# Streamed weight parts: one store each instead of four, a third buffer for them, and one buffer fewer for the packing queries

## The chip, the cores and the metric

The kernel runs on one core of a Trainium2 chip. The metric is the device time of one execution in microseconds (us). The clock of TensorE was granted in full over practically the whole execution (mean 0.999).

## The reference

Three stages in float32, one behind the other. `n_pack` is 32, so 8 heads x 32 queries are packed per batch.

```
def sm_attn(qq, kk, vv):                       # softmax attention, scale 1/8
    ...
p_packed = sm_attn(p, k, v)                    # 8 batches, 8 heads, 32 packing queries, 576 keys, 64 wide
x = sm_attn(q, p_packed, p_packed)             # 576 queries per head against 32 packed values
x = x.transpose(0, 2, 1, 3).reshape(4608, 512)
a, b = x @ w1, x @ w2                          # 512 -> 1024
x = ((a * b) @ w3) @ w_out                     # 1024 -> 1024 -> 512
h = x @ w_in                                   # 512 -> 2048
g = where(h >= 1, h, where(h <= -1, 0, (h + 1) ** 2 / 4))
out = g @ w_out2                               # 2048 -> 512
```

The last stage's matrices are called `win` and `wout` in the kernel; weights arrive as 64-bit floating point words.

## The kernel before, in words

TensorE multiplies "high" and "low" halves: each operand is split into a rounded `hi` (ScalarE copies it into a narrower float type) and the rest `lo` (VectorE subtracts), and each product is made of three matmul passes (`PASSES`).

*Batches.* The first part of the kernel (to about 150 us) converts the weights of the second stage and does the attention of batches 0 and 1. Then a loop over `b` = 1 to 7 does the second stage of batch `b` in 24 units: 16 of `ab_unit` (12 matmuls each: a and b, their product on VectorE, split again) and 8 of `x2_unit` (24 matmuls, one copy on ScalarE, one store to DRAM). After certain units (`EARLY`, `LATE`) come the steps of the attention of batch `b + 1`: scores of packing queries against keys (`scores_k`, units 1 and 3), transposes of their exponentials (`turn_e`, 5 and 7), the product with the values (`packed`, 9) and its transpose (`turn_packed`, 10), scores of the 576 queries (`scores_q`, 12 and 14), and so on. The order in which instructions are written is the order on every engine.

*Weight tasks.* After each unit of batches 1 to 6 stands one task out of `weight_tasks()`, 144 in all. They convert the third stage's matrices and make the seven left sides of Strassen's scheme (A11, A22, S1 to S4, A12) from them, in eight groups of 18 tasks: two groups for `win`, two for `wout`, then the same again. So batch 1 starts with a group for `win`, a second one runs from its end into the middle of batch 2, two for `wout` follow to the end of batch 3, and batches 4 to 6 repeat that. A group has four conversions, sums and differences on VectorE, and up to seven parts. `part(i, a)` takes a buffer `hl` out of a ring (`bufs=2`), has ScalarE write `hi` (L632) and VectorE `lo` (L633), and puts a store on a list. Each store is issued on ScalarE's queue two units later by `flush_weights` (L640), ahead of that unit's task.

*Streamed parts.* Left sides in `STREAM` (S4 and A22) of `win` are not kept on the chip but read back later, one chunk of 128 columns at a time, by `ws_load` out of `wst[n]`, laid out `[partition, chunk, which, k, hi or lo, 128]`. Their eight parts are stored in four transfers each, one for a chunk `c`, because the buffer holds all 512 columns of `hi` and then all of `lo`. Parts of other left sides go out in one transfer.

*Packing queries.* `load_p(b)` brings 32 queries per head for `scores_k`; it is issued on SyncE's queue in `turn_packed` of the batch before, behind `load_v`, from a ring of two. `pb` lies on the same side of the on-chip memory as the `hl` ring.

Tile names in the profile: `hl` the parts' buffers, `ws` and `wi` the DRAM copies of streamed and other parts of `win`, `w` those of `wout`, `cvx` the converted weights, `psk` and `psm` PSUM banks, `ta`, `tb`, `g` the steps of `ab_unit`, `st` the copy of `x2_unit`, `big` the softmax tiles, `pp` the scaled packed values, `pb` the packing queries.

Of the kernel before, what the change touches and what calls it, by code (L numbers as in the profile page):

```python
# [8 lines left out]
F32 = mybir.dt.float32  # L9
F32R = mybir.dt.float32r  # L10
# [3 lines left out]
AF = mybir.ActivationFunctionType  # L14
ALU = mybir.AluOpType
# [7 lines left out]
P = 128  # L23
# [10 lines left out]
STREAM = (S4, A22)  # L34
# [23 lines left out]
def fused_kernel(ctx: ExitStack, tc, qT, kT, vv, pb, w1, w2, w3T, wo, win, wout, out):  # L58
    nc = tc.nc
# [6 lines left out]
    wid = [[dram.tile([P, 2, 2, 512], F32, name=f"wi{i}{n}") for n in range(2)] for i in range(7)]  # L66
    wst = [dram.tile([P, 4, 2, 2, 2, P], F32, name=f"ws{n}") for n in range(2)]
    w2d = [dram.tile([P, 8, 256] if i in PLAIN else [P, 8, 2, 256], F32, name=f"w2{i}") for i in range(7)]
# [14 lines left out]
    a2 = tc.alloc_tile_pool(name="a2", bufs=1, side="left", reuse_waits="tile")  # L83
    cv = tc.alloc_tile_pool(name="cv0", bufs=1, side="left", reuse_waits="tile")
# [24 lines left out]
    def load_weight(pool, src, bufs=1):  # L109

        t = pool.tile([P, 512], src.dtype, name="raw", tag="raw", bufs=bufs)
        nc.sync.dma_start(out=t, in_=src)
        return t

    def as_float32(pool, raw, out, bufs=1, act=False):

        if raw.dtype == F32:
            return lambda: None, lambda: None, lambda: nc.vector.tensor_copy(out=out, in_=raw)  # L120
        quarters = raw.bitcast(U16).rearrange("p (n four) -> p n four", four=4)
        t = pool.tile([P, 512], F32, name="cvt", tag="cvt", bufs=bufs)
        halves = out.bitcast(U16).rearrange("p (n two) -> p n two", two=2)

        def scale():
            nc.scalar.activation(  # L126
                out=t, in_=raw.bitcast(F32).rearrange("p (n two) -> p n two", two=2)[:, :, 1],
                func=AF.Copy, scale=2.0 ** -112)
            if act:
                nc.scalar.activation(  # L130
                    out=halves[:, :, 0], in_=quarters[:, :, 1], func=AF.Copy, scale=2.0 ** -13, bias=-4095.5 / 8192)

        def parts():
            if not act:
                nc.vector.tensor_scalar(
                    out=halves[:, :, 0], in0=quarters[:, :, 1], scalar1=13, scalar2=None,
                    op0=ALU.logical_shift_right)
            nc.vector.tensor_scalar(
                out=halves[:, :, 1], in0=quarters[:, :, 3], scalar1=0x8000, scalar2=None, op0=ALU.bitwise_and)

        def join():
            nc.vector.scalar_tensor_tensor(  # L142
                out=out.bitcast(I32), in0=t.bitcast(I32), scalar=3, in1=out.bitcast(I32),
                op0=ALU.logical_shift_left, op1=ALU.bitwise_or)
        return scale, parts, join
# [20 lines left out]
        loaded["q", b] = t  # L166

    def load_p(b):
        t = a2.tile([P, 2, P], F32, name="pb", tag="pb", bufs=2)
        nc.sync.dma_start(out=t, in_=pb[b])  # L170
        loaded["p", b] = t

# [19 lines left out]
    def attention(b, joint=False):  # L192
# [75 lines left out]
        def turn_packed():  # L268
            def pe():
                c["ps"] = psm()  # L270
                nc.tensor.transpose(c["ps"][:, 0, :P], pp, ident)

            def ew():
                c["ppt"] = a2.tile([P, P], F32, name="ppt", tag="ppt", bufs=1)
                nc.scalar.activation(out=c["ppt"], in_=c["ps"][:, 0, :P], func=AF.Copy)
                if 0 < b < B - 1:
                    load_v(b + 1)
                    load_p(b + 1)
            return pe, ew
# [193 lines left out]
    def convert_end(i):  # L473
        parts[i][1]()
        if i:
            parts[i - 1][2]()
        load_part(i + RAW)
        for f, b in LOADS.get(i, ()):
            {"p": load_p, "k": load_k, "v": load_v}[f](b)
# [80 lines left out]
    cv = tc.alloc_tile_pool(name="cv1", bufs=1, side="left", reuse_waits="tile")  # L560
# [12 lines left out]
    w_stores = []  # L573
# [6 lines left out]
    def weight_tasks():  # L580
        groups = []
        for n in range(2):
            groups += [("in", k, n) for k in range(2)]
            groups += [("out", 2 * n + j, 0) for j in range(2)]
        src = []
        for kind, k, n in groups:
            if kind == "in":
                src += [win[(2 * c + k) * P:(2 * c + k + 1) * P, (2 * r + n) * 512:(2 * r + n + 1) * 512]
                        for r, c in ((0, 0), (0, 1), (1, 0), (1, 1))]
            else:  # L590
                src += [wout[r * P:(r + 1) * P, :] for r in (2 * k, 2 * k + 1, 8 + 2 * k, 9 + 2 * k)]
        src += [None] * 3

        def load(s):
            if s is not None:
                raws.append(load_weight(cv, s, 3))
        for s in src[:3]:
            load(s)
        ahead = src[3:]
        tasks = []  # L600
        for kind, k, n in groups:
            x, q = [], {}

            def convert(y, kind=kind, x=x, q=q):
                def f():
                    if y % 2 == 0:
                        x.append(cv.tile([P, 2, 512], F32, name="cvx", tag="cvx", bufs=2))
                    for a, b in ((0, 0), (0, 1), (1, 0), (1, 1)):
                        if kind == "in" and a < len(x):
                            q[10 * a + b + 11] = x[a][:, b]  # L610
                        if kind == "out" and b < len(x):
                            q[10 * a + b + 11] = x[b][:, :, a * 256:(a + 1) * 256]
                    for g in as_float32(cv, raws.pop(0), x[y // 2][:, y % 2]):
                        g()
                    load(ahead.pop(0))
                return f

            def part(i, a, kind=kind, k=k, n=n, q=q):
                def f():
                    if kind == "out" and i in PLAIN:  # L620
                        w_stores.append((2, lambda: nc.scalar.dma_start(out=w2d[i][:, 2 * k:2 * k + 2], in_=q[a])))
                        return
                    p = cv.tile([P, 1024], F32R, name="hl", tag="hl", bufs=2)
                    if kind == "in":
                        v = p.rearrange("p (v n) -> p v n", v=2)
                        hi, lo = v[:, 0], v[:, 1]
                        v = v.bitcast(F32)
                    else:
                        v = p.rearrange("p (j v n) -> p j v n", j=2, v=2)
                        hi, lo = v[:, :, 0], v[:, :, 1]  # L630
                        v = v.bitcast(F32)
                    nc.scalar.activation(out=hi, in_=q[a], func=AF.Copy)  # L632
                    nc.vector.tensor_tensor(out=lo, in0=q[a], in1=hi.bitcast(F32), op=ALU.subtract)  # L633
                    if kind == "out":
                        to = [(w2d[i][:, 2 * k:2 * k + 2], v)]
                    elif i in STREAM:
                        to = [(wst[n][:, c, STREAM.index(i), k], v[:, :, c * P:(c + 1) * P]) for c in range(4)]
                    else:
                        to = [(wid[i][n][:, k], v)]
                    w_stores.append((2, lambda: [nc.scalar.dma_start(out=d, in_=a) for d, a in to]))  # L640
                return f

            def combine(d, a, b, op, q=q):
                return lambda: nc.vector.tensor_tensor(out=q[d], in0=q[a], in1=q[b], op=op)

            tasks += [
                convert(0), convert(1), part(A11, 11), convert(2), convert(3), part(A22, 22),
                combine(22, 21, 22, ALU.add), part(A12, 12), combine(21, 11, 21, ALU.subtract), part(S1, 22),
                combine(22, 22, 11, ALU.subtract), part(S3, 21), None, part(S2, 22),
                combine(12, 12, 22, ALU.subtract), None, part(S4, 12), None,  # L650
            ]
        return tasks
# [259 lines left out]
    w2_t, rawg, op = {}, {}, {}  # L912
# [102 lines left out]
    for s in range(steps):  # L1015
        t, i = divmod(s, 8)
# [186 lines left out]
```

## Time and profile before

| | |
|---|---|
| time, median of 3 runs | 1292.41 us (1288.88 to 1295.26) |
| the profiled execution: own time | 1291.72 us |
| its span, first to last instruction | 1289.6 us (2.1 us lie around it) |
| TensorE matmuls busy | 1252.4 us, 97% |
| VectorE busy | 864.8 us, 67% |
| ScalarE busy | 698.2 us, 54% |
| transfers | 299.47 MB, mean 232 GB/s |

PE is TensorE's matmul, PEld its weight load, DVE is VectorE, ACT ScalarE, SP SyncE; ACTq and SPq are the instructions that issue transfers, which do not count as busy time. L632 is line 632 of the kernel. In brackets behind a row of a timeline stands how long the engine was idle before it, and what released it, by the profile's own inference.

### The profile page before, as it was taken

To read this page: it belongs to the slowest core of one execution; us is meant where nothing else is said; L and a number is where in the kernel's file an instruction comes from. 1 tells how busy PE (TensorE), PEld (TensorE's weight loads), DVE (VectorE), ACT (ScalarE), POOL (GpSimd) and SP (SyncE) were. 2 spreads that over 40 slices of the span, in tenths; PEclk is the share of its full clock that TensorE was granted. 3 is DMA by queue.
4 is the path that set the end of the run, shared out by engine and by line. 5 is a ranking of instruction groups with operands and counts; after the bars stand their busy time and mean duration, and the time that the engine had idled before them with its cause. 6 is when DMAs were issued, how large, how long until landed. Compare 5 with 4: busy or idle time off the path is not lost.

```text
span 1289.6 us, 21585 instructions
## 1 busy us (share of the span) xinstructions
PE 1252.4 (97%) x8312; PEld 1051.7 (82%) x8312; DVE 864.8 (67%) x1422; ACT 698.2 (54%) x1184; POOL 0.7 (0%) x6
## 2 busy tenths in 40 slices
PE   7989999999989999999999999999999999999998
PEld 3468787989888989998888888888878888888888
DVE  4875776768576769535787787877658546464565
ACT  6774444445545454425676766767755443434443
POOL 0000000000000000000000000000000000000000
PEclk9999999999999999999999999999999999999999
DMA  9773566546456542358767686666999868677675
GB/s 339 279 271 134 190 209 193 189 164 238 144 201 196 207 157 101 101 215 320 271 214 281 212 283 235 230 222 239 351 372 340 332 212 288 215 232 289 212 231 177
DMA packets 131798, 299.47 MB, mean 232 GB/s; under 512 B 11632, under 2 KB 54640, under 8 KB 127216
## 3 DMA queue, kind: packets, MB, share of 16 engines
q1 hardware_dynamic: 92752, 242.91, 54.0%
q10 hardware_dynamic: 38944, 55.19, 12.5%
q8 instruction: 65, 1.06, 0.3%
q14 instruction: 37, 0.30, 0.1%
HBM read 196.21 MB, written 101.84 MB: 231 GB/s over the span
## 4 chain that ended last, share of the span: by engine, by line
PE 69%; DVE 10%; ACT 8%; DMA 8%; issue 3%; ACTq 1%; SPq 0%; DVEq 0%
PE x L1127 14%; PE psk L411 12%; PE x L821 11%; PE psk L387 9%; PE z L1127 6%; PE z L821 5%; PE y L1127 4%; PE y L821 3%; PE psk L493 2%; PE psk L187 2%; ACT r L829 1%; DMA wi<-hl 1%; DMA raw<-w 1%; DVE tb L399 1%; ACT r L832 1%
## 5 line engine op out<-in xcount | busy, mean ns | idle before, releaser
L411 PEld LDWEIGHTS psk<-g,w 128*128 128x128 f32 x1536 | 204.7, 188 | 20.7 <-ACT st L438 6.2
L387 PE MATMUL psk<-at,m 128*128 128x288 f32 x1536 | 219.4, 299 | 1.8 <-ACT ta L397 1.5
L387 PEld LDWEIGHTS psk<-at,m 128*128 128x128 f32 x1536 | 207.4, 189 | 14.3 <-issue 8.4
L411 PE MATMUL psk<-g,w 128*128 128x288 f32 x1536 | 211.3, 297 | 5.1 <-ACT st L438 2.7
L821 PE MATMUL x<-x2s,wi 128*128 128x512 f32 (+1 forms) x720 | 163.2, 371 | 1.8 <-ACT m L894 1.2
L983 DVE TENSOR_TENSOR op<-raw,op 128x1024 fp32r<-128x1024 f32 (+1 forms) x94 | 101.8, 1113 | 70.6 <-ACT op L982 70.4
L821 PEld LDWEIGHTS x<-x2s,wi 128*128 128x128 f32 x720 | 125.7, 188 | 27.9 <-ACT m L894 3.9
L982 ACT ACTIVATE op<-raw 128x1024 fp32r<-128x1024 f32 (+1 forms) x94 | 87.4, 966 | 70.6 <-DVE raw L974 32.3
L1127 PE MATMUL x<-op,w 128*128 128x512 f32 (+1 forms) x480 | 100.5, 369 | 0.4 <-DVE op L983 0.3
L1127 PE MATMUL x<-op,hwi 128*128 128x512 f32 (+1 forms) x480 | 100.6, 369 | 0.0
L1127 PEld LDWEIGHTS x<-op,w 128*128 128x128 f32 x480 | 83.8, 188 | 16.3 <-DVE op L983 1.3
L1127 PEld LDWEIGHTS x<-op,hwi 128*128 128x128 f32 x480 | 83.1, 188 | 16.1 <-DVE op L983 0.4
L399 DVE TENSOR_TENSOR tb<-psk,ta 128x288 f32<-128x288 f32 x128 | 57.8, 453 | 54.5 <-ACT ta L397 35.0
L832 ACT ACTIVATE r<-r 128x1024 f32<-128x1024 f32 (+1 forms) x80 | 78.0, 975 | 2.5
L983 DVE TENSOR_TENSOR op<-r,op 128x1024 fp32r<-128x1024 f32 (+1 forms) x46 | 50.2, 1117 | 38.7 <-ACT op L982 38.5
L835 DVE SCALAR_TENSOR_TENSOR U<-U,r 128x512 f32<-128x512 f32 (+1 forms) x80 | 47.4, 634 | 38.3 <-ACT r L832 38.3
L493 PE MATMUL psk<-wo,w3f 128*128 128x512 f32 x128 | 60.2, 621 | 10.9 <-DVE w3f L142 10.8
L894 ACT ACTIVATE m<-x 128x512 f32<-128x512 f32 (+1 forms) x40 | 22.1, 553 | 80.4 <-PE x L821 44.8
L105 ACT ACTIVATE g<-tb 128x288 fp32r<-128x288 f32 x128 | 56.3, 439 | 14.7 <-DVE tb L399 14.7
L126 ACT ACTIVATE cvt<-raw 128x512 f32<-128x512 f32 x72 | 48.7, 676 | 28.3 <-DMA raw<-w3T 7.8
L982 ACT ACTIVATE op<-r 128x1024 fp32r<-128x1024 f32 (+1 forms) x46 | 43.2, 969 | 38.1 <-DVE L L1104 16.2
L397 ACT ACTIVATE ta<-psk 128x288 f32<-128x288 f32 x128 | 51.1, 402 | 21.9 <-PE psk L387 21.8
(111 smaller groups left out, 1858.4 us busy)
## 6 DMA issues: line engine op xcount, KB each, us to landing
raw<-g SPq DMA_DIRECT2D x86, 512.0 KB, 5.2
g<-L SPq DMA_DIRECT2D x64, 512.0 KB, 3.8
r<-g SPq DMA_DIRECT2D x42, 512.0 KB, 5.2
g<-U SPq DMA_DIRECT2D x64, 256.0 KB, 2.1
ws<-ws SPq DMA_DIRECT2D x42, 256.0 KB, 4.3
x2d<-st ACTq DMA_DIRECT2D x72, 144.0 KB, 2.4
v<-vv SPq DMA_DIRECT2D x8, 1280.0 KB, 7.5
wi<-hl ACTq DMA_DIRECT2D x20, 512.0 KB, 3.3
```

What stands on the lines that cost most here:

```text
L105: nc.scalar.activation(out=dst[:, 0], in_=src, func=AF.Copy)
L126: nc.scalar.activation(out=t, in_=raw.bitcast(F32).rearrange("p (n two) -> p n two", two=2)[:, :, 1], func=AF.Copy, scale=2.0 ** -112)
L387: nc.tensor.matmul(ps[w][:, :HS], m_tile[b, w, n][:, s, G, c0 * P:(c0 + 1) * P], at_tile[b][:, G, v, hf * HS:(hf + 1) * HS], start=(k == 0 ...
L397: nc.scalar.activation(out=bs, in_=ps[1][:, :HS], func=AF.Copy)
L399: nc.vector.tensor_tensor(out=g, in0=ps[0][:, :HS], in1=bs, op=ALU.mult)
L411: nc.tensor.matmul(ps, w34[kt][:, s, mt * P:(mt + 1) * P], g_t[kt, hf][:, v, :], start=(kt == kts[0] and n == 0), stop=(kt == kts[-1] and ...
L493: nc.tensor.matmul(acc[4 * hf + m], w3f[hf, j][:, m * P:(m + 1) * P], wof[j], start=(j == 0), stop=(j == 7))
L821: nc.tensor.matmul(bank[s, b][:, :N], w, x2_t[t, q][:, m, k, :N], start=(j == 0 and q in (A11, S1, A12)), stop=(j == 5), skip_group_check= ...
L832: nc.scalar.activation(out=r, in_=r, func=AF.Square)
L982: nc.scalar.activation(out=o[:, :, 0, :N], in_=a[0], func=AF.Copy)
L983: nc.vector.tensor_tensor(out=o[:, :, 1, :N], in0=a[0], in1=o[:, :, 0, :N].bitcast(F32), op=ALU.subtract)
L1127: nc.tensor.matmul(bank[b][d][:, :N], w2_t[q][j // 2][:, 2 * (j % 2) + k, s, d * P:(d + 1) * P], op[x][:, k, v, :N], start=start and k == ...
```

## The change

Three edits. The buffer of a streamed part is laid out chunk by chunk (128 columns of `hi`, then the same 128 of `lo`, four times), both split instructions write it so, and it is stored in one transfer with four runs of 1 KB per partition. The ring `hl` has three buffers, not two. The ring `pb` has one, not two.

```
     def load_p(b):
-        t = a2.tile([P, 2, P], F32, name="pb", tag="pb", bufs=2)
+        t = a2.tile([P, 2, P], F32, name="pb", tag="pb", bufs=1)
...
-                    p = cv.tile([P, 1024], F32R, name="hl", tag="hl", bufs=2)
-                    if kind == "in":
+                    p = cv.tile([P, 1024], F32R, name="hl", tag="hl", bufs=3)
+                    whole = q[a]
+                    if kind == "in" and i in STREAM:
+                        v = p.rearrange("p (c v n) -> p c v n", c=4, v=2)
+                        hi, lo = v[:, :, 0], v[:, :, 1]
+                        whole = whole.rearrange("p (c n) -> p c n", c=4)
+                        v = p.bitcast(F32).rearrange("p (c n) -> p c n", c=4)
+                    elif kind == "in":
...
-                    nc.scalar.activation(out=hi, in_=q[a], func=AF.Copy)
-                    nc.vector.tensor_tensor(out=lo, in0=q[a], in1=hi.bitcast(F32), op=ALU.subtract)
+                    nc.scalar.activation(out=hi, in_=whole, func=AF.Copy)
+                    nc.vector.tensor_tensor(out=lo, in0=whole, in1=hi.bitcast(F32), op=ALU.subtract)
                     if kind == "out":
-                        to = [(w2d[i][:, 2 * k:2 * k + 2], v)]
+                        to = w2d[i][:, 2 * k:2 * k + 2]
                     elif i in STREAM:
-                        to = [(wst[n][:, c, STREAM.index(i), k], v[:, :, c * P:(c + 1) * P]) for c in range(4)]
+                        to = wst[n][:, :, STREAM.index(i), k].rearrange("p c v n -> p c (v n)")
                     else:
-                        to = [(wid[i][n][:, k], v)]
-                    w_stores.append((2, lambda: [nc.scalar.dma_start(out=d, in_=a) for d, a in to]))
+                        to = wid[i][n][:, k]
+                    w_stores.append((2, lambda: nc.scalar.dma_start(out=to, in_=v)))
```

## Rows read from the trace of the kernel before

**Rows 1.** The chain of work that ended last, by engine, share of the span.

```profile
PE 69%; DVE 10%; ACT 8%; DMA 8%; issue 3%; ACTq 1%; SPq 0%; DVEq 0%
```

**Rows 2.** Busy time by stretch: PE, PEld, DVE, ACT, POOL; clock, DMA share, GB/s.

```profile
151.00:510.00 359.00, 344.84 (x3399) 313.27 (x3398) 264.28 (x555) 176.97 (x408) 0.00 (x0) 1.00 0.54 186
...
184.00:211.00 27.00, 27.00 (x238) 23.89 (x237) 22.43 (x42) 13.20 (x27) 0.00 (x0) 1.00 0.42 133
278.00:309.10 31.10, 31.10 (x349) 28.79 (x349) 23.12 (x55) 17.86 (x44) 0.00 (x0) 1.00 0.60 206
340.00:374.00 34.00, 30.47 (x337) 27.23 (x336) 24.42 (x56) 17.66 (x43) 0.00 (x0) 1.00 0.76 249
243.00:263.00 20.00, 18.38 (x156) 16.50 (x154) 16.08 (x34) 9.00 (x19) 0.00 (x0) 1.00 0.61 210
```

**Rows 3.** Timeline of TensorE: start, duration, what, [idle before, releaser].

```profile
171.08 0.33 PE L271 MATMUL psm<-ident,pp 128*128 128x128 f32 x1 [1.57 <-DVE pp L262]
...
181.58 12.96 PE L411 MATMUL psk<-g,w 128*128 128x288 f32 x96 [0.86 <-ACT ta L397]
...
224.76 1.45 PE L228 MATMUL psm<-ident,big 128*116 128x128 f32 x8 [2.15 <-ACT big L212]
...
246.72 8.46 PE L411 MATMUL psk<-g,w 128*128 128x288 f32 x62 [0.24 <-ACT ta L397]
...
262.93 6.61 PE L411 MATMUL psk<-g,w 128*128 128x288 f32 x48 [1.38 <-ACT st L438]
...
361.59 0.33 PE L271 MATMUL psm<-ident,pp 128*128 128x128 f32 x1 [0.84 <-DVE pp L262]
...
369.53 3.46 PE L387 MATMUL psk<-at,m 128*128 128x288 f32 x24 [1.49 <-ACT ta L397]
374.05 1.19 PE L411 MATMUL psk<-g,w 128*128 128x288 f32 x7 [1.05 <-ACT ta L397]
...
416.31 1.09 PE L228 MATMUL psm<-ident,big 128*116 128x128 f32 x8 [1.24 <-ACT big L212]
```

**Rows 4.** Timeline of ScalarE (ACT) and its queue (ACTq), same columns.

```profile
164.50 2.85 ACTq L640 DMA_DIRECT2D ws<-hl  x3
167.40 0.63 ACT L632 ACTIVATE hl<-cvx 128x512 fp32r<-128x512 f32 x1 [2.61 <-DMA ws<-hl]
...
169.22 0.34 ACTq L640 DMA_DIRECT2D wi<-hl  x1
...
176.08 0.63 ACT L632 ACTIVATE hl<-cvx 128x512 fp32r<-128x512 f32 x1 [3.03 <-DMA wi<-hl]
...
216.54 1.85 ACTq L640 DMA_DIRECT2D ws<-hl  x2
...
219.50 0.63 ACT L632 ACTIVATE hl<-cvx 128x512 fp32r<-128x512 f32 x1 [2.18 <-issue]
...
243.65 2.01 ACTq L640 DMA_DIRECT2D ws<-hl  x4
...
368.55 0.63 ACT L632 ACTIVATE hl<-cvx 128x512 fp32r<-128x512 f32 x1 [4.99 <-DMA wi<-hl]
```

**Rows 5.** Instructions by tile: duration ns min/median/max, first and last start us.

```profile
L632 ACT ACTIVATE hl<-cvx x40: 614/630/652, 154.7 to 503.3; 128x512 fp32r<-128x512 f32 x40
...
L640 ACTq DMA_DIRECT2D ws<-hl x32: 377/500/1572, 164.1 to 435.1; - x32
...
L664 SPq DMA_DIRECT2D f<-x2d x5: 518/530/615, 522.3 to 827.2; - x5
```

**Rows 6.** Transfers: queue, count, KB each, median us from issue to landing.

```profile
wi<-hl ACTq DMA_DIRECT2D x20, 512.0 KB, 3.3
...
ws<-hl ACTq DMA_DIRECT2D x32, 128.0 KB, 2.1
```

**Rows 7.** Timelines of TensorE and SyncE's queue (SPq): packing queries.

```profile
153.63 0.72 PE L187 MATMUL psm<-qk,pb 64*32 64x288 f32 x16 [0.48 <-ACT big L212]
...
168.15 0.45 SPq L170 DMA_DIRECT2D pb<-pb  x1
```

## The prediction

> **What bounds the kernel now.** I read the chain of waits first, then the engines by stretch, then TensorE's own timeline wherever it stands still, and last ScalarE's timeline just before those places. The chain says that TensorE carries 69% of the span, and VectorE, ScalarE and transfers some 8 to 10% each [rows 1]: matmuls set the time, except at spots where another engine holds them up. The change touches only the weight tasks of batches 1 to 6, which run from 151 to 510 us. There TensorE is busy for 344.8 of 359.0 us [rows 2]. So 14.2 us of its idle time are all that can be won; what leaves ScalarE, VectorE or a queue elsewhere is worth nothing.
>
> Eleven of these idle spells (12.4 us) stand in six places [rows 3]; I name them by batch. A is batch 1 (171.08, 181.58), B and C batch 2 (224.76; 246.72 and 262.93), D batch 4 (361.59, 369.53, 374.05), E and F batch 5 (416.31; and two spells that repeat C's to 0.01 us and are not shown). B and C repeat as E and F, and A as D, because the weight groups repeat every three batches. In batch 3, whose tasks convert only the second matrix, TensorE never stops although VectorE works 23.1 of 31.1 us [rows 2]: the stalls belong to the groups with streamed parts.
>
> Two things on ScalarE's timeline stand before them [rows 4].
> - *The four issues.* At A three of the four transfers of one streamed part take 2.85 us to issue, and the split that follows in ScalarE's stream starts at 167.40, 3.3 us after the first of the four. At B it starts at 219.50, 2.96 us after the first issue at 216.54. At C the four take 2.01 us.
> - *The ring of two.* At 176.08 a split has waited 3.03 us for a store of the part two before it, and at 368.55 4.99 us. The first of these stores was issued at 169.22, so it took 6.8 us beside the load of the next batch's values; the median of such 512 KB stores is 3.3 [rows 6].
>
> **The change part by part.**
>
> *Four issues become one.* Eight streamed parts, so 32 issues become 8. One quarter part takes 0.50 us to issue in the median, 0.38 at least, 1.57 at most [rows 5]; it has 256 contiguous runs of 512 bytes on the SBUF side. The merged transfer has 128 x 4 runs of 1 KB. ScalarE issues nothing with 512 runs in the trace. The bounds: below, 0.34 us, what it takes to issue a part of another product, one run per partition [rows 4]; above, the four issues as they are, 2.0 us at C and 3.3 at A. The nearest row is the load of the third stage's activations, f, four runs per partition and so 512 too, although on SP's queue: 0.53 us [rows 5]. I take 0.53. What it gives at each place is the smaller of the time saved and the stall:
> - A, first stall: from 164.1 to the end of the last issue, 164.50 + 2.85 = 167.35, it is 3.25 us; ScalarE comes to the split 3.25 - 0.53 = 2.7 us sooner. Behind that split wait two evacuations of TensorE's products, then on VectorE the low half, two products and the scaling of the packed values, which TensorE waits for. The stall is 1.57: gone.
> - D, first stall, the same chain: at least 4 x 0.50 - 0.53 = 1.47 us sooner, stall 0.84: gone.
> - B: VectorE's maximum of the next scores stands behind the low half of that split, then the exponential, then TensorE's transposes. 2.96 - 0.53 = 2.4 us sooner, stall 2.15: gone. E, the same chain: 1.47 sooner, stall 1.24: gone. These four make 1.57 + 0.84 + 2.15 + 1.24 = 5.80 us.
> - C: 2.01 - 0.53 = 1.48 us sooner, against 0.24 + 1.38 = 1.62 of stall. The second of these comes 16 us after the issues; between them a chain of VectorE's work runs, which is busy 16.1 of the 20 us from 243 to 263 [rows 2]. If it starts sooner by 1.48 and nothing in it is bound by something else, it ends sooner by 1.48; if something is, by nothing. I take the half, 0.74, and keep both ends. F the same: 0.74. Together 1.48, from 0 to 2.96.
>
> The two other streamed parts leave around 196 and 388 us, in the second half of a batch, where TensorE is never idle (184 to 211 us [rows 2]): nothing.
>
> *Two buffers become three.* The split at 176.08 then takes the buffer of the streamed part two tasks earlier still, issued from 164.1 on [rows 5]. Even at the 6.8 us of a late store it lands by 171.5 (164.1 and 0.53 and 6.8), ahead of the split's own turn at 173.05 (176.08 less the wait). So both waits vanish, and with them the second stall of A (0.86) and the second and third of D (1.49 + 1.05), which follow each other on one chain: the evacuation behind the late split, the maximum and subtraction on VectorE, the exponential, the next evacuation. Sum 3.40 us. Next in line there is VectorE, which would work its 24.4 us in about 34.0 - 3.4 = 30.6 [rows 2]: 80%, against 74% in batch 3. That is no stall by itself, but little slack; a rival below has it otherwise.
>
> *One buffer for the packing queries.* The load of the next batch's queries now waits for the last scores that read this batch's. These are computed at 153.63; the load is issued at 168.15 [rows 7], 14 us later, behind work that depends on those scores. The wait is over before it begins: 0. Behind it on SP stands only the next load of keys, which is issued later yet.
>
> *The shape of the split.* Its two instructions write four pieces of 128 columns instead of one of 512, for 8 of 40 splits. No row has that shape; the splits of the second matrix, in two pieces of 256, lie in the same 0.61 to 0.65 us as all the rest [rows 5], so 0, and at most the spread of 0.04 us on each of 16 instructions, 0.6 us off TensorE's path for the most part. The DRAM layout, the loads that read it and the matmuls are as before.
>
> **The sum.** 5.80 + 1.48 + 3.40 = 10.7 us, from the profiled execution's own 1291.72: 1281.0 us. The median of the runs shown is 1292.41, so the profiled one stands for them to 0.05%. With both unknowns at their better end, 5.80 + 2.96 + 3.40 = 12.2: 1279.6.
>
> The row at C shows four issues at 2.01 us, with 2.1 as the median landing of one such quarter [rows 4, 6]: issuing takes as long as moving. The Trainium skill, "DMA: Bandwidth & Descriptors", section "Issuing engines are not separate DMA queues", says that the sequencer's time to initiate a transfer is usually small relative to the transfer; by that rule fewer issues would save nothing here, and the sum would be the 3.40 of the third buffer. The trace does not agree with it at this size.
>
> **The rivals.**
> 1. *One transfer holds ScalarE as long as four.* If the hold follows the bytes or other traffic and not the number of issues, only the third buffer counts: 1291.7 - 3.4 = 1288.3, no measurable change. For it: four equal issues took from 2.01 to 3.3 us, so something besides their number matters. Against it: that load of 512 runs is issued in 0.53, and a whole 512 KB part of another product in 0.34 [rows 4, 5]. Chance 0.15.
> 2. *VectorE comes next.* If its in-order work keeps what the third buffer and C and F would give, 5.80 are left: 1285.9, on the edge of what can be told. For it: 80% busy there after the gain, and ScalarE's evacuation behind an exponential that waits for VectorE. Against it: batch 3, the same attention steps without a stall. Chance 0.10.
> 3. *The merged transfer blocks ScalarE until most of it has moved: slower.* Place: the six above, price: at 6.8 us (the late store) instead of 2.74 (mean of 3.25, 2.96 and 2.01), 6 x 4.06 = 24.4 us lost, 3.4 won: 1312.7. It decides for slower once one issue holds for more than 4.4 us (6 x 1.65 = 3.4 + 6.5). For it: single issues of 1.57 us exist. Against it: none of 32 is longer. Chance 0.05.
>
> **How the numbers follow.** The forecast, all of the four stalls and the third buffer and about half of C and F, has 0.70. Within 0.5% of 1292.4, or 6.5 us, a measurement of this kernel can hardly tell a change (its three runs lie 6.4 apart). The forecast is faster by that bound, rival 1 same, rival 2 half and half, rival 3 slower: 0.75, 0.20, 0.05. The range goes from the better end, 1279.6, less some 2.6 for the spread of runs, to rival 1's 1288.3 and a little over: 1277 to 1289.
>
> **What would show it.** After the change, 8 issues of the streamed store at about 0.53 us each and in no place over 1; no split that waits for a store of a part; TensorE idle for about 14.2 - 10.7 = 3.5 us in this stretch, with nothing before the transposes of batches 2 and 5, the scaled values of 1 and 4, and the first products after the attention steps. I am wrong if the issues take 2 us or more, if the same stalls appear with VectorE as the releaser, or if the time won here is lost after 510 us, where nothing changes but the start.

## The result and the profile after

The changed kernel takes 1277.76 us in the median of 6 runs (1274.46 to 1278.83), the kernel before 1295.76 in 6 (1288.88 to 1296.83). The ratio is 0.9869 (95%: 0.9849 to 0.9890), so about 17 us or 1.3% faster (the medians are 18.0 apart). The forecast was 1281.0 with a range of 1277 to 1289.

The two profiled executions are 1291.72 and 1278.23 us, 13.5 apart. I measure the part that the change touches from landmark to landmark: from the first stall of batch 1 (the second scores of packing queries, 153.63 us before [rows 7]) to the last of batch 5 (F's second, at 452.93 before, C's counterpart). It took 299.30 us and takes 284.11 after, 156.21 to 440.32: 15.2 us less. The last landmark before, then both after:

```profile
452.93 6.64 PE L411 MATMUL psk<-g,w 128*128 128x288 f32 x48 [1.37 <-ACT st L438]
```
```profile
156.21 0.72 PE L187 MATMUL psm<-qk,pb 64*32 64x288 f32 x16 [0.53 <-ACT big L212]
...
440.32 4.89 PE L411 MATMUL psk<-g,w 128*128 128x288 f32 x35 [0.39 <-ACT st L438]
```

Ahead of it the profile after is 2.6 us later, behind it 0.6 us shorter. The lateness is no effect of the change: in the eleven profiles of this study the first landmark lies anywhere from 153.4 to 156.2, 153.6 and 155.2 in the two of the unchanged kernel.

The chain of the kernel after, by engine, then its stretch of weight tasks (columns as in [rows 2]), then what TensorE waited for there: us in total, times, longest.

```profile
PE 78%; DVE 7%; DMA 7%; ACT 5%; issue 2%; ACTq 0%; SPq 0%; DVEq 0%
```
```profile
151.00:500.00 349.00, 346.41 (x3456) 315.42 (x3462) 267.55 (x561) 179.17 (x414) 0.00 (x0) 1.00 0.56 195
```
```profile
PE psm L228 <- ACT big L212: 1.3, 2, 1.1
PE psk L411 <- ACT st L438: 0.8, 2, 0.4
PE psm L187 <- ACT big L212: 0.5, 1, 0.5
```

TensorE's share of the chain rises from 69% [rows 1] to 78%. Its idle time in the stretch falls from 14.2 us [rows 2] to 349.0 - 346.4 = 2.6; some 3.5 were forecast. Of the eleven stalls of the prediction only the second of C and of F are left, 0.39 us each. The 1.3 and the 0.5 are spells of 1.08, 0.53 and 0.20 us ahead of the streamed stores, and were there before.

The tile view after has the issues (durations ns min/median/max, first and last start) and what the two instructions of each split waited for (us, times; the 13.4 us are VectorE's, which waits for ScalarE's half):

```profile
L638 ACT ACTIVATE hl<-cvx x40: 614/623/652, 157.2 to 490.7; 128x512 fp32r<-128x512 f32 x40
...
L646 ACTq DMA_DIRECT2D ws<-hl x8: 526/532/599, 166.6 to 422.5; - x8
...
  ACT hl L638: 13.4, 12
  DVE cvx L142: 7.4, 6
  ACT st L438: 1.8, 4
```

Eight issues of 0.53 us in place of 32 of 0.50 [rows 5], none over 0.60. No split waits for a store of a part; before, two waited 3.03 and 4.99 us [rows 4]. At places A and B the timelines after have no stall to show:

```profile
171.93 0.27 PE L271 MATMUL psm<-ident,pp 128*128 128x128 f32 x1
...
181.37 1.90 PE L411 MATMUL psk<-g,w 128*128 128x288 f32 x13
...
222.13 1.09 PE L228 MATMUL psm<-ident,big 128*116 128x128 f32 x8
```
```profile
216.20 0.53 ACTq L646 DMA_DIRECT2D ws<-hl  x1
216.79 0.19 ACT L212 ACTIVATION_READ_ACCUMULATOR big<-psm,nb 128x1 f32 x1
216.88 0.62 ACT L638 ACTIVATE hl<-cvx 128x512 fp32r<-128x512 f32 x1
```

At B the split now starts 0.68 us after the first issue, not 2.96 [rows 4], and the transposes follow without the 2.15 us of idle time [rows 3].

### The profile page after: what moved, and what is told of

Read it like the earlier page. It is cut to its first block, busy times and chain, and to the rows that moved or that the text cites. A ratio compares the mean times of both kernels' runs of the same rounds, so it can differ in the third digit from the quotient of the medians.

```text
span 1276.4 us, 21545 instructions
## 1 busy us (share of the span) xinstructions
PE 1250.6 (98%) x8312; PEld 1051.9 (82%) x8312; DVE 864.3 (68%) x1422; ACT 697.5 (55%) x1184; POOL 0.7 (0%) x6
## 4 chain that ended last, share of the span: by engine, by line
PE 78%; DVE 7%; DMA 7%; ACT 5%; issue 2%; ACTq 0%; SPq 0%; DVEq 0%
PE x L1133 15%; PE x L827 13%; PE psk L387 13%; PE psk L411 13%; PE z L1133 7%; PE z L827 7%; PE y L1133 4%; PE y L827 4%; PE psk L187 2%; DMA raw<-w3T 1%; DMA raw<-wo 1%; DMA ws<-ws 1%; DMA raw<-w 1%; ACT cvt L126 1%; DVE tb L399 1%
## 5 line engine op out<-in xcount | busy, mean ns | idle before, releaser
L411 PEld LDWEIGHTS psk<-g,w 128*128 128x128 f32 x1536 | 204.8, 188 | 15.5 <-ACT st L438 6.0
L387 PE MATMUL psk<-at,m 128*128 128x288 f32 x1536 | 216.7, 298 | 0.0
L438 ACT ACTIVATE st<-psk 128x288 f32<-128x288 f32 x64 | 26.1, 407 | 67.5 <-PE psk L411 67.1
```

Source lines behind the costliest of these rows:

```text
L387: nc.tensor.matmul(ps[w][:, :HS], m_tile[b, w, n][:, s, G, c0 * P:(c0 + 1) * P], at_tile[b][:, G, v, hf * HS:(hf + 1) * HS], start=(k == 0 ...
L411: nc.tensor.matmul(ps, w34[kt][:, s, mt * P:(mt + 1) * P], g_t[kt, hf][:, v, :], start=(kt == kts[0] and n == 0), stop=(kt == kts[-1] and ...
```

## The experiments

Theory: four issues hold ScalarE's stream, and the evacuations behind them come late. Rivals: the ring of two is what mattered, or the form of the transfers. Each run is told with its time against the kernel before on the same chip (medians of 1293.99, 1293.17 and 1293.89 us on the three chips used), and with the length of the stretch between the two landmarks, which leaves out what varies ahead and behind (299.30 in the kernel before). A gain in time below is taken from the ratio.

| kernel | time us | ratio (95%) | stretch us |
|---|---|---|---|
| before again | 1294.69 | 0.9999 (0.9983 to 1.0015) | 300.29 |
| one buffer for the queries alone | 1294.11 | 0.9998 (0.9980 to 1.0015) | 298.45 |
| third buffer (and one for the queries) | 1288.58 | 0.9950 (0.9934 to 0.9967) | 293.81 |
| merged store alone | 1279.46 | 0.9880 (0.9856 to 0.9905) | 284.26 |
| four short transfers | 1285.91 | 0.9944 (0.9925 to 0.9963) | 293.10 |
| eight short transfers | 1304.31 | 1.0087 (1.0064 to 1.0110) | not taken |
| four on SyncE's queue, two buffers | 1279.91 | 0.9893 (0.9871 to 0.9915) | 287.96 |
| merged, two buffers, other stores on SyncE | 1281.04 | 0.9909 (0.9888 to 0.9930) | 286.52 |
| merged, three buffers, other stores on SyncE | 1277.98 | 0.9882 (0.9863 to 0.9901) | 284.03 |

**The merged store alone.** From the changed kernel:

```
-                    p = cv.tile([P, 1024], F32R, name="hl", tag="hl", bufs=3)
+                    p = cv.tile([P, 1024], F32R, name="hl", tag="hl", bufs=2)
...
-        t = a2.tile([P, 2, P], F32, name="pb", tag="pb", bufs=1)
+        t = a2.tile([P, 2, P], F32, name="pb", tag="pb", bufs=2)
```

> Only the merged store of a streamed part; the ring keeps two buffers and the packing queries two. Theory (the four issues hold ScalarE): the first stalls of A and D and those of B, C, E and F go, with the half-speed clock behind B; the waits of the splits for a store of the part two before it stay, and with them the second stall of A and the second and third of D, about 3.4 us. So 10 to 12 us faster than before, 4 us short of the full change. Rival (the ring of two is what matters, an issue is cheap): at most 2 us faster, and the stalls before the transposes of batches 2 and 5 are still there.

The first half of the theory held, the second missed. All of B, E and both first stalls went, but so did those that I had put down to the ring: the gain is 15.5 us where 10 to 12 were expected, and the stretch is that of the full change. Its timeline around the waits of batch 1 (transfers' issues, and the splits):

```profile
166.75 0.33 ACTq L646 DMA_DIRECT2D wi<-hl  x1
...
167.50 0.33 SPq L175 DMA_DIRECT2D v<-vv  x1
...
169.83 0.63 ACT L638 ACTIVATE hl<-cvx 128x512 fp32r<-128x512 f32 x1 [2.64 <-DMA ws<-hl]
...
172.03 0.63 ACT L638 ACTIVATE hl<-cvx 128x512 fp32r<-128x512 f32 x1
```

The store of A12 is issued 0.75 us ahead of the load of the next batch's values and lands 4.0 us later; before it was issued 1.45 us behind that load (169.22 [rows 4] against 167.77) and took 6.8. So the split of S3 (172.03) waits for nothing. The ring of two still makes another split wait 2.64 us, and no stall follows. The load of the values in the kernel before:

```profile
167.77 0.33 SPq L175 DMA_DIRECT2D v<-vv  x1
```

The order of these two transfers separates the cases in every profile with two buffers that issues A12's store on ScalarE's queue. In seven places (batches 1 and 4 of the kernel before, of its second profile and of the single buffer for the queries; batch 4 of the run on SyncE's queue below) the store was issued 0.17 to 1.45 us behind the load, landed 6.8 to 9.3 us later, and S3's split waited 3.0 to 5.5 us. In three (both batches here, batch 1 of that run) it was issued 0.50 to 0.75 us ahead, landed 3.2 to 4.2 us later, and the split did not wait. No run changes this order alone.

**The third buffer, with one buffer for the queries.** From the kernel before:

```
-        t = a2.tile([P, 2, P], F32, name="pb", tag="pb", bufs=2)
+        t = a2.tile([P, 2, P], F32, name="pb", tag="pb", bufs=1)
...
-                    p = cv.tile([P, 1024], F32R, name="hl", tag="hl", bufs=2)
+                    p = cv.tile([P, 1024], F32R, name="hl", tag="hl", bufs=3)
```

> Only the third buffer and the single buffer for the packing queries; four issues per streamed part as before. Theory: no split waits for a store any more, the second stall of A and the second and third of D go, 3.4 us by the idle rows and about 4 with the matmul that drains before each stall; A's first stall and B, C, E, F stay as they are. Rival (the ring is the main thing): 10 us or more faster, with B and E gone too.

As expected: the stalls behind the late splits are gone from A and D, the others stand (B's at 2.01, E's at 1.24, C's and F's at 1.36 and 1.38). The stretch is 5.5 us shorter, the time 6.5. Some 1.6 us of the 5.5 are a spell at a lower clock behind B, which the kernel before has in its profile and this one has not (shown at the end of the section after this one).

**The kernel before again, and one buffer for the queries alone.** The latter differs from the kernel before only in `bufs=1` of `pb`.

> The kernel before, unchanged, for a second profile. Theory: the eleven stalls stand at the same places and within 0.3 us of their size, a stall of over 2 us at B is followed by a stretch at half the granted clock, and the first 150 us differ from one execution to the next by some 2 us, because they wait for loads. Rival (the stalls move about by chance): fewer than eight of the eleven come back. Ratio to before 1.000 within 0.002.

> Only the single buffer for the packing queries. Theory: no load waits for it, ratio to before 1.000 within 0.003, the same stalls. Rival (the load comes late without its second buffer): the maximum of the scores or the scores themselves wait for the queries' load, and the time grows by 2 us or more.

All eleven places stalled again, eight of them within 0.2 us of their size. D's first and second moved by 0.3 and 0.5 (0.50 and 1.96). A's first shrank from 1.57 to 0.53, because the four issues held ScalarE 2.2 us there instead of 3.3 (the table of holds below), and a stall of 1.54 stood between A's two, as D has one. The single buffer for the queries changes nothing that can be measured. It frees 1 KB of each partition on the side where the third part buffer takes 4 KB more; whether the third would fit without it no run here shows.

**Four and eight short transfers.** Both from the changed kernel, with three buffers. The first stores the four chunks one by one (one run of 1 KB per partition each), the second `hi` and `lo` of each apart (512 bytes):

```
+                    if kind == "in" and i in STREAM:
+                        w_stores.append((2, lambda: [nc.scalar.dma_start(out=to[:, c], in_=v[:, c]) for c in range(4)]))
+                    else:
+                        w_stores.append((2, lambda: nc.scalar.dma_start(out=to, in_=v)))
-                    w_stores.append((2, lambda: nc.scalar.dma_start(out=to, in_=v)))
```
```
+                    if kind == "in" and i in STREAM:
+                        w_stores.append((2, lambda: [nc.scalar.dma_start(out=to[:, c, h * P:(h + 1) * P],
+                            in_=v[:, c, h * P:(h + 1) * P]) for c in range(4) for h in range(2)]))
...
```

> The changed kernel, but each streamed part leaves again in four transfers, one run of 1 KB per partition each. Theory (the hold on ScalarE sets the stalls, and an issue costs by its runs plus a part of its own): four issues of 0.33 us hold ScalarE for 1.3 us instead of 0.53, so at B, where 2.96 us gave a stall of 2.15, about 0.5 us come back, at E (2.0 us gave 1.24) about 0.5, at C and F 0.8 each, at A and D nothing; 2 to 3 us slower than the changed kernel, 12 to 14 us faster than before. Rival (the number of issues alone counts, or the runs alone): the stalls are back in full, 5 us faster than before, or none is back.

> The changed kernel with eight transfers per streamed part, one run of 512 bytes per partition each. Theory (the hold on ScalarE sets the stalls): eight issues of 0.33 us hold it for 2.6 us, between what the old form held it at E and at B, so with three buffers it comes out as the third buffer alone did, 5 to 8 us faster than before, with stalls of 1.8 us or so before the transposes of batches 2 and 5. Rival (the transfers' many short runs did the harm by loading the DMA engines, not the issuing): 128 runs per issue and fewer held-up issues, so at most half of those stalls, and 10 us or more faster than before.

Both misses taught the price. I had reckoned 0.33 us an issue from stores that are issued singly. Only the first of several is that cheap; the median is 0.45 and 0.44 in the two, against 0.50 for 256 runs, so what counts is mostly the number of issues, not their runs. Four short ones hold ScalarE 1.8 to 3.1 us and give 7 us, with stalls back at A, D, B and E and the second ones of C and F at 1.39 and 1.40. Eight hold it 3.7 to 6.1, more than the old form, and make the kernel 11 us slower than before: its eight stalls sum to 17.9 us against 12.4, and behind several the granted clock fell (0.50 from 371 to 375 us, behind D's). Place A in the two, ScalarE's queue and then TensorE:

```profile
164.85 1.68 ACTq L647 DMA_DIRECT2D ws<-hl  x3
...
170.26 0.33 PE L271 MATMUL psm<-ident,pp 128*128 128x128 f32 x1 [0.35 <-DVE pp L262]
```
```profile
166.47 5.74 ACTq L647 DMA_DIRECT2D ws<-hl  x7
...
175.94 0.48 PE L271 MATMUL psm<-ident,pp 128*128 128x128 f32 x1 [4.39 <-DVE pp L262]
```

Over all kernels that issue on ScalarE, the hold (start of a part's first issue to the end of its last) and TensorE's next stall, in us:

| kernel | A hold, stall | D hold, stall | B hold, stall | E hold, stall |
|---|---|---|---|---|
| before | 3.27, 1.57 | 2.50, 0.84 | 2.91, 2.15 | 2.00, 1.24 |
| before again | 2.23, 0.53 | 2.15, 0.50 | 2.88, 2.12 | 1.99, 1.23 |
| queries alone | 2.24, 0.54 | 2.44, 0.79 | 2.81, 2.06 | 2.01, 1.24 |
| third buffer | 3.30, 1.59 | 2.86, 1.20 | 2.78, 2.01 | 2.00, 1.24 |
| four short | 2.04, 0.35 | 2.30, 0.65 | 3.07, 2.31 | 1.80, 1.04 |
| eight short | 6.11, 4.39 | 4.39, 2.75 | | |
| after | 0.60, 0 | 0.54, 0 | 0.53, 0 | 0.53, 0 |

At each place the stall is the hold less a constant, to 0.03 us: 1.70 at A, 1.65 at D, 0.76 at B and E. That constant is the slack of the chain behind the issues. (With eight, B and E split into two stalls and are left out; C and F are not in the table.) This settles the cause at these four places: the hold sets the stall, whatever the transfers are made of.

**Four transfers on SyncE's queue.** The kernel before, with two buffers and the same 32 transfers:

```
-                    w_stores.append((2, lambda: [nc.scalar.dma_start(out=d, in_=a) for d, a in to]))
+                    w_stores.append((2, lambda: [(nc.sync if len(to) > 1 else nc.scalar).dma_start(out=d, in_=a) for d, a in to]))
```

> The kernel before with the same four transfers for each streamed part and two buffers, but these issued on SyncE's queue instead of ScalarE's. Theory (the harm is ScalarE's time): the stalls of B and E and the first of A and D go although the transfers are the same, C and F shrink to 0.4, and as with the merged store alone the ring of two hurts no more; 12 to 16 us faster than before. Rival (the form of the transfers matters, or SyncE's loads are held up behind the stores): less than 8 us faster, with waits for loads of weights or of values in place of the old ones.

The time is as the theory had it, 14 us faster with the old transfers, so their form did no harm by itself. What TensorE waited for, and the late split of batch 4:

```profile
PE psk L387 <- ACT ta L397: 1.7, 1, 1.7
...
PE psk L411 <- ACT ta L397: 1.1, 1, 1.1
```
```profile
353.34 0.35 SPq L175 DMA_DIRECT2D v<-vv  x1
...
353.51 0.33 ACTq L640 DMA_DIRECT2D wi<-hl  x1
...
362.54 0.63 ACT L632 ACTIVATE hl<-cvx 128x512 fp32r<-128x512 f32 x1 [5.19 <-DMA wi<-hl]
```

The part on the ring missed: in batch 4 A12's store came 0.17 us behind the load of the values, and D's second and third stalls are there; of its first, 0.31 is left. In batch 1 it came ahead, and A has no stall:

```profile
169.54 0.33 ACTq L640 DMA_DIRECT2D wi<-hl  x1
170.22 0.35 SPq L175 DMA_DIRECT2D v<-vv  x1
...
175.19 0.63 ACT L632 ACTIVATE hl<-cvx 128x512 fp32r<-128x512 f32 x1
```

So with a ring of two the store can fall behind that load without the four issues on ScalarE.

**Two and three buffers with the other stores on SyncE.** Both from the changed kernel, the first with the two ring sizes of before:

```
-                    w_stores.append((2, lambda: nc.scalar.dma_start(out=to, in_=v)))
+                    eng = nc.sync if kind == "in" and i not in STREAM else nc.scalar
+                    w_stores.append((2, lambda: eng.dma_start(out=to, in_=v)))
```

> The merged store with two buffers, and the stores of the other parts of the first matrix issued on SyncE's queue, so that in batches 1 and 4 the store of A12 always stands behind the load of the next batch's values and queries instead of racing it from ScalarE's queue. Theory (with two buffers the wait of the split at S3 is decided by whether that store gets ahead of the load): behind it, the store lands 6 us or more after its issue, the split waits 3 to 5 us in batches 1 and 4, and TensorE's stalls of 1 to 2 us behind it are back in at least one of them; 2 to 4 us slower than the merged store with two buffers on ScalarE's queue. Rival (a merged store leaves ScalarE so far ahead that a wait there is hidden whatever the order): the waits are there, but TensorE has no stall in batches 1 and 4.

> The same with three buffers. Theory: the stores land as late, but no split waits for one and TensorE has no stall in batches 1 and 4; as fast as the changed kernel within 2 us. Rival (the order on SyncE's queue itself costs, loads held up behind stores): 3 us or more slower than the changed kernel, with TensorE or the conversions waiting for loads.

The premise of the first was wrong: A12's store stands ahead of the load on that queue too (354.27 against 355.02 in batch 4). But A11's, one part earlier, now lands late, and with two buffers it is A12's split that waits for it, ahead of the scaling that TensorE waits for. Splits and TensorE with two buffers:

```profile
168.55 0.63 ACT L638 ACTIVATE hl<-cvx 128x512 fp32r<-128x512 f32 x1 [1.96 <-DMA wi<-hl]
...
352.89 0.63 ACT L638 ACTIVATE hl<-cvx 128x512 fp32r<-128x512 f32 x1 [2.15 <-DMA wi<-hl]
```
```profile
172.23 0.33 PE L271 MATMUL psm<-ident,pp 128*128 128x128 f32 x1 [0.91 <-DVE pp L262]
...
356.56 0.33 PE L271 MATMUL psm<-ident,pp 128*128 128x128 f32 x1 [1.09 <-DVE pp L262]
```

With three buffers neither wait nor stall is there, and the stretch is the 284 us of the changed kernel. So a wait of the ring of two is not hidden in general, as the rival would have it. It depends on which split waits: in the merged store alone 2.64 us of waiting came behind the scaling and cost nothing, here 1.96 us ahead of it end in a stall of 0.91. The first of the two kernels is 2.3 us of stretch slower than the merged store with the stores on ScalarE's queue (286.52 against 284.26); 2 to 4 were expected.

## Why the prediction was right, and where its sum was not

- *The bound.* Right as to the place, TensorE's stalls of 151 to 510 us. Wrong as a ceiling: 14.2 us of idle time were called all that can be won, and the stretch lost 15.2 us with 2.6 us of idle time left. Some of TensorE's busy time went too (*The sum*).
- *The issues.* Right in mechanism and in price: 0.53 us was taken, from a load on another queue, and 0.53 measured. A's and D's first stalls, B and E went in full, as reckoned (5.80 us by the idle rows).
- *C and F.* The half was too little: 0.24 + 1.38 became 0 + 0.39 at C, and F alike. That is 1.23 of the 1.48 each, so 2.5 us instead of 1.5. VectorE's chain of 16 us passes nearly all of the time on.
- *The third buffer.* The step that failed is its 3.40 us as a term of its own. Alone it takes away just these stalls, 3.40 us by the idle rows and about 4 of stretch; on top of the merged store it gives 284.26 - 284.11 = 0.15, nothing that can be measured. The waits were late stores', and the merged store removes them too: with it A12's store gets ahead of the load of the values and lands in 4.0 us, not 6.8. The two edits remove the same stalls, so their gains do not add. The sum does not show the error, since the stalls are counted once; that they went is no evidence for the third buffer.
- *The sum.* 10.7 was forecast, 15.2 came in the stretch. The time, 1277.76, is in the range by 0.8 us, and that is luck: the low end had been set by a better end of 1279.6 and the spread of runs, without the two terms that follow. The idle rows account for 12.42 - 0.78 = 11.6 of the gain, of which C and F are 1.0 more than reckoned. Two things were left out. One is the granted clock behind B. The other is that an idle row is not the whole stall: a matmul of 128x288 is shown as 0.30 us (row below) although they follow each other at 3.44 / 24 = 0.14, so the end of the last one before a stall covers part of it. From the first product of the second half of batch 4 to that of batch 5 the kernel before needed 436.70 - 374.05 = 62.65 us and the one after 425.17 - 364.41 = 60.76, 1.89 less, for idle rows of 1.24 + 0.23 = 1.47: 0.2 a stall. By this estimate nine vanished stalls make 1.9 us; with the 1.57 of the clock below, 11.6 becomes 15.1.

```profile
L387 PE MATMUL psk<-at,m 128*128 128x288 f32 x1536 | 219.4, 299 | 1.8 <-ACT ta L397 1.5
```

- *The rivals.* One transfer holding ScalarE as long as four: refuted by 0.53. VectorE next: refuted, 0.39 left at C and F is all. The merged transfer blocking ScalarE: refuted, at most 0.60. The Trainium skill, "DMA: Bandwidth & Descriptors", section "Issuing engines are not separate DMA queues", calls the time to initiate a transfer usually small relative to the transfer. For a single quarter the trace has 0.50 us of issue [rows 5] against 2.1 to landing [rows 6], a quarter of it; the prediction set four issues, 2.0 us, against one landing. What the runs refute is the conclusion drawn from it there, that fewer issues would save nothing: the merged store alone takes 15.0 us from the stretch, because the four issues add up on ScalarE, ahead of its evacuations.

As to the clock, the windows behind B in the kernel before (column before the last two: granted clock), then its products:

```profile
225.00:229.00 4.00, 4.00 (x22) 4.00 (x21) 3.45 (x7) 3.66 (x9) 0.00 (x0) 0.57 0.57 236
229.00:233.00 4.00, 4.00 (x32) 4.00 (x32) 2.96 (x9) 2.39 (x6) 0.00 (x0) 1.00 0.31 131
```
```profile
225.86 4.71 PE L387 MATMUL psk<-at,m 128*128 128x288 f32 x24
...
230.55 3.44 PE L387 MATMUL psk<-at,m 128*128 128x288 f32 x24
```

Behind the 2.15 us of waiting the clock stood at its lower level, 1.2 GHz, for most of 4 us, and 24 products took 4.71 us instead of 3.44. From B's transposes to the first product of the second half it took 246.72 - 224.76 = 21.96 us, from E's 436.70 - 416.31 = 20.39: the spell cost 1.57 us. The unchanged kernel's second profile has it too (21.93, clock 0.57 in 228 to 232); those with only one buffer for the queries and only the third buffer have a stall of 2.06 and 2.01 at B, no spell, and 20.38 both. The stall's length does not decide it alone: with eight transfers the clock fell behind a stall of 1.94 us (0.57 from 254 to 258) and not behind one of 2.42 (1.00 from 232 to 236). So it is a price that only some of these stalls pay.

## What to carry to other kernels

Where a compute engine issues transfers, its time per issue (here 0.33 to 0.53 us for a single one, 0.44 to 0.50 in the median for several in a row) stands in the stream of evacuations: compare the hold with the slack of what waits behind it, and merge or move the issues where the hold is longer. A wait for a buffer may be the child of such a hold, when a store that is issued late gets behind other loads; price two such edits by their shared stalls, not by their sum. And count a stall of TensorE as the idle row, plus the matmul that drains before it, plus a possible spell at the lower clock.

## What was not expected of the hardware

Issues in a row cost more than a single one, 0.45 against 0.33 us with one run per partition. In some places one of several takes 1.2 to 1.7 us, though the DMA engines are idle for much of it. At B in the kernel before the second of the four issues lasted from about 216.9 to 218.4; the DMA share there (tenths, 40 slices of 0.1 us from 216 on) was

```profile
DMA  0000000070000038887310001000049998589996
```

The engines stood idle from 216.9 to 217.4 and nearly so again around 218, and the short issues with half the runs had long ones too (1.72 us at most). In E and C no such long one came in any profile; in A, B and D of the same kernel it came in some.

One thing in the traces goes with the long ones. The eleven profiles have 198 issues of streamed stores that follow another in a row, and eleven of them take over 1 us (one on SyncE's queue). Beside each of the eleven runs an instruction load, a transfer of 16 KB on the queue q8 that begins at most 0.4 us before or after the issue does. Of the other 187 only two have one about so near (0.40 and 0.42 us later), and they take 0.59 and 0.73 us. The DMA share above shows it at 216.8. The queues in the holds of B and C in the kernel before (216.5 to 219.5 and 243.65 to 245.66; packets, MB, share of the engines):

```profile
q10 hardware_dynamic: 553, 0.27, 30.7%
q8 instruction: 1, 0.02, 2.4%
```
```profile
q10 hardware_dynamic: 539, 0.26, 45.6%
```

At A the kernel before has such a load in its hold of 3.27 us; its second profile, with a hold of 2.23, has none. Fourteen single issues, or first ones of a row, had such a load as near and stayed under 0.55 us, the merged one of 216.20 after among them (0.53). That the load is the cause is not shown: no run here moves it, and whose instructions it brings is open. The other issues of 0.6 to 0.9 us are open too.
